# A long convolution and a token mixer on one Trainium2 core: step one's last tile copied in two operations, step two's last sums in halves, and two chunks' sums of group 4 on VectorE

## The chip, the cores and the metric

The kernel runs on one core of a Trainium2 chip. The core has five engines with a queue of instructions each: TensorE (PE, its weight loads shown as PEld), VectorE (DVE), ScalarE (ACT), GpSimd (POOL) and SyncE (SP), which issues most of the transfers between HBM and the on-chip memory SBUF. TensorE writes its results to a second on-chip memory, PSUM, from which VectorE and ScalarE read. The metric is the device time of one launch in microseconds, as the median of several runs.

## The reference

```python
x = A_q                                                   # 2048 tokens, 640 channels
sa, ca, ga, sb, cb, gb = (silu(c) @ w_mod).reshape(6, 640)
h = layernorm(x) * (1 + ca) + sa
k_shift = causal depthwise convolution of A_k with A_shift_k, 4 taps
kv = k_shift * A_v
y = irfft(rfft(kv, 4096) * rfft(A_ssm_k, 4096))[:2048]    # a long causal convolution per channel
x = x + ga * (h * (y + kv * A_ssm_D))
h = layernorm(x) * (1 + cb) + sb
u = gelu(einsum("sd,sf->df", h, B_w1) + B_b1)
out = x + gb * (einsum("df,fs->ds", u, B_w2) + B_b2).T
```

## The kernel before

The 640 channels are worked in five chunks of 128, `c` = 0 to 4 (the loop at L521). A chunk's long convolution is done as products with Fourier matrices on TensorE:

- **Step one**, `step1(side, t)` at L222: sixteen products of a tile of the kv side (`side` 0, from the buffer `X`) or of the ssm_k side (`side` 1, from the buffer `P`) go to one PSUM slot. ScalarE then copies the slot into `Z`, laid out by side, tile, row, column and half. There are four tiles `t` a side, and a tile has 64 columns `k1` for each row.
- **Step two**, `f2(g)` at L236, for eight groups `g` of eight columns: 32 products read the columns 8g to 8g + 7 of all eight tiles of `Z`. ScalarE copies the filter's half of the result to `kt` (L250). Two products on VectorE (`mul`, L254) multiply it with the signal's half into `pa` and `pb`, which lie in `P` and are used by every second group. Two sums (`add`, L260) then make the real and the imaginary part of `Y`, for the eight columns and all 32 rows `i`. The sums are GpSimd's, except those of group 7, which are VectorE's in the chunks from 1 on (L552).
- **Back**, `i2(r)` at L267 and `i1(half)` at L285: `i2(0)` reads the rows 0 to 15 of `Y` in all columns, `i2(1)` the rows 16 to 31; ScalarE (in the last chunk VectorE too, L281) copies the results to `T2`. `i1` gives half of the tokens, and `gate` multiplies them with the normalised input; the result is added to x.

Every engine works off its instructions in the order in which the program issues them; there is no scheduler. In the loop over `g` (L525 to L548) VectorE gets the products of group g - 1, GpSimd (L530) the sums of group g - 2, ScalarE two operations on the input, and VectorE a share of a list `fill`: the short convolution and the product with v for a later chunk, or statistics. After the loop come the products of group 7, the sums of group 6 on GpSimd and the sums of group 7. Then follow, for chunks 1 to 3, two tiles of step one for the next chunk, a copy on ScalarE that permutes ssm_k into `P` (L176), seven operations of `fill`, `i2(0)`, two operations on the whole chunk's input (`po`, L303), further tiles of step one, `i2(1)` and `i1`. Chunk 4 has, in place of the next chunk's work, modulation products (L358) and the first splits of the mixer's weights (L418). In chunks 1 to 3, GpSimd also adds `ssm_D` to a row of ssm_k (L173) after group 3.

PSUM has three slots that go round (`ring`, L69), so group g of step two can write its slot when the products of group g - 3 have read it. A fourth slot holds the running sum of the short convolution and its taps. VectorE's operations of the short convolution read one operand from there and one from SBUF; its sums for `Y` read both operands from SBUF.

From about 292 us on the second normalisation and the token mixer follow, in two large matrix products.

Of the kernel before, what the change touches and what calls it, by code (L numbers as in the profile page):

```python
# [11 lines left out]
AF = mybir.ActivationFunctionType  # L12
ALU = mybir.AluOpType
# [37 lines left out]
def mixer_kernel(ctx: ExitStack, tc: tile.TileContext, q, k, v, shift_k, ssm_k, ssm_D, w1, b1, w2, b2, c,  # L51
# [7 lines left out]
    act, dve, pool, pe, sync = nc.scalar, nc.vector, nc.gpsimd, nc.tensor, nc.sync  # L59
    TT = lambda eng, o, a, b, op: eng.tensor_tensor(o, a, b, op=op)  # L60
# [36 lines left out]
    Z = T_z.rearrange("p (s t a k e) -> p s t a k e", s=2, t=4, a=8, e=2)  # L97
    T2 = T_z[:, 4096:8192].rearrange("p (a m e) -> p a m e", a=32, e=2)
    Y = T_y.rearrange("p (r i k) -> p r i k", r=2, i=32)
# [122 lines left out]
    def step1(side, t, later=False):  # L222

        ps = psum()
        for a in range(8):
            i = 8 * t + a
            lhs = KSP[:, i] if side else X.rearrange("p (m i) -> p i m", i=32)[:, i]
            o = 512 * (a % 2) + 128 * (a // 2)
            for ri in range(2):
                pe.matmul(ps[64 * ri:64 * ri + 64, o:o + 128], lhs, F1[:, 128 * ri:128 * ri + 128], start=True,  # L230
                          stop=True)
        evac = lambda: act.activation(Z[:, side, t].rearrange("p a k e -> p e a k"),  # L232
                                      ps.rearrange("p (e a k) -> p e a k", a=8, e=2), AF.Copy)
        return evac if later else evac()

    def f2(g):  # L236

        ps = psum()
        for kk in range(8):
            k1 = 8 * g + kk  # L240
            for ri in range(2):
                for h in range(2):
                    o = 128 * kk + 64 * ri
                    rhs = bass.AP(tensor=T_z.tensor, offset=T_z.offset + 128 * h + 2 * k1,
                                  ap=[T_z.ap[0], [256, 32], [1, 2]])
                    pe.matmul(ps[64 * h:64 * h + 64, o:o + 64], W2[k1 // 32][:, 2 * (k1 % 32) + ri], rhs, start=True, stop=True)  # L246
        pv = ps.rearrange("p (m s i) -> p m s i", s=2, i=32)
        xs_ = pv[:, :, 0]
        kt = KT[g % 2]
        act.activation(kt.rearrange("p (m i) -> p m i", i=32), pv[:, :, 1], AF.Copy)  # L250
        pa, pb = P[:, 1024 * (g % 2):1024 * (g % 2) + 512], P[:, 1024 * (g % 2) + 512:1024 * (g % 2) + 1024]
        m16 = lambda t: t.rearrange("p (m i) -> p m i", i=32)

        def mul():  # L254
            TT(dve, m16(pa), xs_, m16(kt), ALU.mult)
            sw = bass.AP(tensor=kt.tensor, offset=kt.offset + 32, ap=[kt.ap[0], [64, 8], [-32, 2], [1, 32]])
            TT(dve, pb.rearrange("p (k r i) -> p k r i", k=8, r=2), xs_.rearrange("p (k r) i -> p k r i", r=2), sw,
               ALU.mult)

        def add(eng=pool):  # L260
            for ri, t, op in ((0, pa, ALU.subtract), (1, pb, ALU.add)):
                t = t.rearrange("p (k r i) -> p r i k", k=8, r=2)
                TT(eng, Y[:, ri, :, 8 * g:8 * g + 8], t[:, 0], t[:, 1], op)
        return mul, add


# [254 lines left out]
    for c in range(NC):  # L521
# [3 lines left out]
        for g in range(8):  # L525
# [1 line left out]
            if pend_m:  # L527
                pend_m()
            if pend_a:
                pend_a()  # L530
            pend_a, pend_m = (pend_m and pa_next), m_
            pa_next = a_
            if c:
# [15 lines left out]
        pend_m()  # L549
        if pend_a:  # L550
            pend_a()
        pa_next(dve if c else pool)  # L552
        if c == 0:
            for j in range(16):
                for h in range(2):
# [6 lines left out]
        if c == 0:  # L562
# [3 lines left out]
            ps = psum()  # L566
# [45 lines left out]
        else:  # L612
# [6 lines left out]
            t = mem("in", 4288, "wb3")  # L619
# [4 lines left out]
        if c:  # L624
            dv(7 if cn is not None else 8)
            i2(0)
            if cn is None:
                mod_part(tap, 3, pl[3])
                i2(1, dve)
                t = mem("y", 4096, "wb2")  # L630
# [19 lines left out]
        for half in range(2):  # L650
            ps = i1(half)
# [123 lines left out]
    ps = i1(1, s1)  # L775
# [405 lines left out]
```

## Time and profile before

| | us |
|---|---|
| median of 3 runs | 689.63 (688.66 to 690.23) |
| the profiled execution's own time | 686.98 |
| its span, from the first to the last instruction | 685.2 |
| PE busy | 631.4 |
| DVE busy | 513.5 |
| ACT busy | 313.7 |
| POOL busy | 147.1 |

The page says who was busy and for how long, and its chain of waits says who ended last, followed back from the last instruction. A line of a timeline gives start, length, engine, line, operation, output and inputs, how many instructions were merged, and in brackets the idle time of the engine before and who ended it. Names stand without their numbers: `z` is `Z`, `y` is `Y`, `p` is the buffer `P`, `pst` a PSUM slot. All of VectorE's and GpSimd's two-operand operations have the line of one helper, L60, and are told apart by their tiles. Step two runs at about 42, 104, 157, 206 and 257 us in the five chunks.

### The profile page before, as it was taken

The page shows a single profiled execution, that of the slowest core. Times are in us where ns is not written, and L with a number is a line of the kernel's source. Part 1 is how long each engine was busy: PE and PEld are TensorE (multiplying, and loading weights), DVE is VectorE, ACT ScalarE, POOL GpSimd, SP SyncE. Part 2 cuts the span into 40 slices and gives each one's busy share as a digit, 9 for nine tenths or more (in the row PEclk, how much of TensorE's full clock was granted, in tenths as well). Part 3 has the DMA queues.
Part 4 walks back from the last instruction along what each step waited for, and adds up shares of the span by engine and source line. Part 5 has one row for each costly group of instructions (what it writes and reads, how often), then busy time and mean ns, then how long its engine had stood idle before and what let it go on. Part 6 is the DMA issues. An engine that isn't in the chain of part 4 may idle for free.

```text
span 685.2 us, 20698 instructions
## 1 busy us (share of the span) xinstructions
PE 631.4 (92%) x9057; PEld 613.1 (89%) x9057; DVE 513.5 (75%) x865; ACT 313.7 (46%) x469; POOL 147.1 (21%) x120
## 2 busy tenths in 40 slices
PE   0699888989999989997799999999999999999997
PEld 0699688989999989787799999999999999999997
DVE  7677689969879737888996320774589888888886
ACT  0564674735745645555777321532433332333331
POOL 5298048525526427200000000000000000000000
PEclk9999989999999999989999999999999999999999
DMA  9978988546432623352112750577589563355511
GB/s 184 215 219 242 357 154 173 121 80 147 77 63 85 178 48 81 118 127 60 29 34 57 129 112 12 139 186 193 167 300 347 170 182 103 117 168 170 175 40 40
DMA packets 173552, 95.91 MB, mean 140 GB/s; under 512 B 89715, under 2 KB 163222, under 8 KB 173462
## 3 DMA queue, kind: packets, MB, share of 16 engines
q1 hardware_dynamic: 168914, 93.28, 52.5%
q10 hardware_dynamic: 4548, 1.31, 1.1%
q8 instruction: 71, 1.16, 0.7%
q14 instruction: 19, 0.16, 0.1%
HBM read 77.53 MB, written 17.04 MB: 138 GB/s over the span
## 4 chain that ended last, share of the span: by engine, by line
PE 69%; DVE 15%; POOL 5%; DMA 3%; issue 2%; SPq 2%; ACT 2%; ACTq 0%; POOLq 0%; DVEq 0%
PE pst L1082 25%; PE pst L441 19%; PE pst L230 8%; PE pst L246 6%; PE pst L275 5%; POOL y L60 4%; PE pst L947 3%; DVE tap L60 2%; PE pst L294 2%; DVE kt L60 2%; SPq L166 2%; DMA in<-in_A_k_dram 1%; POOL t L60 1%; DMA aux<-in_A_ssm_k_dram 1%; DVE p L60 1%
## 5 line engine op out<-in xcount | busy, mean ns | idle before, releaser
L246 PEld LDWEIGHTS pst<-z,w 128*64 128x64 f32 x2560 | 94.8, 141 | 9.2 <-ACT z L232 7.3
L246 PE MATMUL pst<-z,w 128*64 128x64 f32 x2560 | 96.0, 240 | 7.5 <-ACT z L232 6.1
L60 POOL TENSOR_TENSOR y<-p 128x256 f32<-128x256 f32 x72 | 92.0, 1339 | 25.0 <-DVE p L60 24.6
L60 DVE TENSOR_TENSOR p<-pst,kt 128x512 f32<-128x512 f32 x80 | 52.5, 693 | 21.0 <-ACT kt L250 15.1
L230 PE MATMUL pst<-v,x 128*64 128x128 f32 x640 | 45.5, 302 | 23.4 <-DVE x L60 23.4
L230 PEld LDWEIGHTS pst<-v,x 128*64 128x64 f32 x640 | 43.6, 221 | 23.9 <-POOL aux L60 23.3
L232 ACT ACTIVATE z<-pst 128x1024 f32<-128x1024 f32 x40 | 46.4, 1165 | 39.3 <-PE pst L230 19.4
L250 ACT ACTIVATE kt<-pst 128x512 f32<-128x512 f32 x40 | 25.1, 628 | 49.5 <-PE pst L246 27.3
L275 PEld LDWEIGHTS pst<-v,y 32*128 32x128 f32 x1280 | 38.0, 187 | 5.4 <-POOL y L60 2.5
L275 PE MATMUL pst<-v,y 32*128 32x64 f32 x1280 | 39.9, 272 | 2.5 <-DVE y L60 1.4
L230 PE MATMUL pst<-v,p 128*64 128x128 f32 x640 | 37.3, 274 | 2.1 <-ACT p L176 1.1
L230 PEld LDWEIGHTS pst<-v,p 128*64 128x64 f32 x640 | 35.0, 137 | 3.1 <-issue 1.5
L1082 PE MATMUL pst<-r_z,m_w 128*128 128x320 f32 x198 | 37.1, 309 | 0.0
L60 DVE TENSOR_TENSOR tap<-tap,kt 128x512 f32<-128x512 f32 x51 | 35.6, 697 | 1.3
L60 DVE TENSOR_TENSOR kt<-in,tap 128x512 f32<-128x512 f32 x51 | 35.0, 687 | 1.5
L1082 PEld LDWEIGHTS pst<-r_z,m_w 128*128 128x128 f32 x198 | 31.1, 188 | 0.0
L283 ACT ACTIVATE z<-pst 128x512 f32<-128x512 f32 x38 | 21.5, 667 | 20.2 <-PE pst L275 20.2
L1019 ACT ACTIVATE m_w<-m_v 128x896 fp32r<-128x896 f32 x19 | 17.9, 948 | 23.3 <-DVE m_v L60 13.1
L294 PEld LDWEIGHTS pst<-z,v 64*64 64x64 f32 x1280 | 22.6, 146 | 6.6 <-issue 3.6
L294 PE MATMUL pst<-z,v 64*64 64x64 f32 x1280 | 24.6, 231 | 3.1 <-issue 2.1
L60 DVE TENSOR_TENSOR m_w<-m_v,m_w 128x896 fp32r<-128x896 f32 x19 | 20.7, 1087 | 6.5 <-ACT m_w L1019 6.5
L60 DVE TENSOR_TENSOR aux<-pst,aux 128x1024 f32<-128x1024 f32 (+2 forms) x11 | 12.3, 1125 | 16.6 <-PE pst L294 16.6
(300 smaller groups left out, 1434.9 us busy)
## 6 DMA issues: line engine op xcount, KB each, us to landing
x<-in_B_w_dram SPq DMA_DIRECT2D x20, 512.0 KB
m_v<-in_B_w_dram SPq DMA_DIRECT2D x20, 384.0 KB
aux<-in_A_ssm_k_dram SPq DMA_DIRECT2D x10, 512.0 KB
out_dram<-m_w SPq DMA_DIRECT2D x32, 160.0 KB
in<-in_A_k_dram SPq DMA_DIRECT2D x36, 128.0 KB
in<-in_A_v_dram SPq DMA_DIRECT2D x36, 128.0 KB
ts<-m_p SPq DMA_DIRECT2D x10, 320.0 KB
m_w<-xs SPq DMA_DIRECT2D x20, 160.0 KB
```

What stands on the lines that cost most here:

```text
L60: TT = lambda eng, o, a, b, op: eng.tensor_tensor(o, a, b, op=op)
L230: pe.matmul(ps[64 * ri:64 * ri + 64, o:o + 128], lhs, F1[:, 128 * ri:128 * ri + 128], start=True, stop=True)
L232: evac = lambda: act.activation(Z[:, side, t].rearrange("p a k e -> p e a k"), ps.rearrange("p (e a k) -> p e a k", a=8, e=2), AF.Copy)
L246: pe.matmul(ps[64 * h:64 * h + 64, o:o + 64], W2[k1 // 32][:, 2 * (k1 % 32) + ri], rhs, start=True, stop=True)
L250: act.activation(kt.rearrange("p (m i) -> p m i", i=32), pv[:, :, 1], AF.Copy)
L275: pe.matmul(pp[qd // 2][:, o:o + 64], Y[p, ri, i:i + 2].rearrange("p i k -> p (i k)"), V2[p, 64 * ri:64 * ri + 64], start=ri == 0, stop=ri ...
L283: act.activation(o, i, AF.Copy)
L294: pe.matmul(ps[64 * b:64 * b + 64, 512 * e + 64 * jj:512 * e + 64 * jj + 64], V1[p, ri, n2], T2[p, :, 32 * ri + n2], start=ri == 0, stop=r ...
L441: pe.matmul(ps[0:m, h, 0:320], w_.bitcast(F32R), r_[:, 320 * h:320 * h + 320].bitcast(F32R), start=first and i == 0, stop=last and i == 2)
L947: pe.matmul(ps[n][:, h, 0:320], sets[n][:, j].bitcast(F32R), r[:, 320 * h:320 * h + 320].bitcast(F32R), start=j == 0 and r is hh, stop=j = ...
L1019: act.activation(W[n][0].bitcast(F32R), A[p, w_], AF.Copy)
L1082: pe.matmul(bank[n], w[:, i].bitcast(F32R), r.bitcast(F32R), start=m == 0 and k == 0, stop=m == 6 and k == 2)
```

## The change

Three edits. First, `step1`'s copy of the ssm_k side's last tile (`side` 1, `t` 3) is made in two operations, columns 0 to 7 and then 8 to 63, in all five chunks. Second, in the chunks from 1 on the sums of group 7 are made for the rows 0 to 15 first, real and imaginary, and then for the rows 16 to 31: four operations on VectorE in place of two. Third, in chunks 2 and 3 the sums that are issued in the loop at `g` = 6, those of group 4, go to VectorE and no longer to GpSimd.

```diff
@@ step1
-        evac = lambda: act.activation(Z[:, side, t].rearrange("p a k e -> p e a k"),
-                                      ps.rearrange("p (e a k) -> p e a k", a=8, e=2), AF.Copy)
+        def evac(cuts=(0, 8, 64) if side and t == 3 else (0, 64)):
+
+            for k0, k1 in zip(cuts, cuts[1:]):
+                act.activation(Z[:, side, t, :, k0:k1].rearrange("p a k e -> p e a k"),
+                               ps.rearrange("p (e a k) -> p e a k", a=8, e=2)[:, :, :, k0:k1], AF.Copy)
         return evac if later else evac()
@@ f2
-        def add(eng=pool):
-            for ri, t, op in ((0, pa, ALU.subtract), (1, pb, ALU.add)):
-                t = t.rearrange("p (k r i) -> p r i k", k=8, r=2)
-                TT(eng, Y[:, ri, :, 8 * g:8 * g + 8], t[:, 0], t[:, 1], op)
+        def add(eng=pool, parts=(slice(0, 32),)):
+            for i in parts:
+                for ri, t, op in ((0, pa, ALU.subtract), (1, pb, ALU.add)):
+                    t = t.rearrange("p (k r i) -> p r i k", k=8, r=2)
+                    TT(eng, Y[:, ri, i, 8 * g:8 * g + 8], t[:, 0, i], t[:, 1, i], op)
@@ the loop over g
             if pend_a:
-                pend_a()
+                pend_a(dve if c in (2, 3) and g == 6 else pool)
@@ after the loop
-        pa_next(dve if c else pool)
+        if c:
+            pa_next(dve, (slice(0, 16), slice(16, 32)))
+        else:
+            pa_next()
```

VectorE at the end of step two in chunk 3, before and after (chunk 2 is alike; `p<-pst` are the two products of a group, `y<-p` its sums, `x<-tap,in` the last operation of `fill`, and the rows behind the sums the statistics of x):

```order
L60 TENSOR_TENSOR p<-pst_3081,kt 128x512 x2
L60 TENSOR_TENSOR x<-tap,in 128x512
L60 TENSOR_TENSOR p<-pst_3122,kt 128x512 x2
L60 TENSOR_TENSOR p<-pst_3163,kt 128x512 x2
L60 TENSOR_TENSOR p<-pst_3203,kt 128x512 x2
L60 TENSOR_TENSOR y<-p 128x32x8 x2
L520 BN_STATS sm<-xa 128x6 x7
```

```order
L60 TENSOR_TENSOR p<-pst_3089,kt 128x512 x2
L60 TENSOR_TENSOR x<-tap,in 128x512
L60 TENSOR_TENSOR p<-pst_3130,kt 128x512 x2
L60 TENSOR_TENSOR y<-p 128x32x8 x2
L60 TENSOR_TENSOR p<-pst_3171,kt 128x512 x2
L60 TENSOR_TENSOR p<-pst_3211,kt 128x512 x2
L60 TENSOR_TENSOR y<-p 128x16x8 x4
L524 BN_STATS sm<-xa 128x6 x7
```

The two sums of group 4 now stand between the products of group 5 and those of group 6, and the sums of group 7 are four operations of 16 rows.

ScalarE at the passage from step one to step two in chunk 4, before and after (`z<-pst` are the copies of step one's tiles, `kt<-pst` the first copy of step two, `aux` the input's normalisation):

```order
L232 ACTIVATE z<-pst_3658 128x2x512
L232 ACTIVATE z<-pst_3676 128x2x512
L250 ACTIVATE kt<-pst_3706 128x512
L301 ACTIVATE aux<-xa,sm 128x128 x2
L538 ACTIVATE x<-sm 128x1
```

```order
L235 ACTIVATE z<-pst_3668 128x2x512
L235 ACTIVATE z<-pst_3686 128x2x8x8
L235 ACTIVATE z<-pst_3686 128x2x8x56
L253 ACTIVATE kt<-pst_3717 128x512
L305 ACTIVATE aux<-xa,sm 128x128 x2
L542 ACTIVATE x<-sm 128x1
```

The last tile's copy is now two operations, of 2 x 8 x 8 and of 2 x 8 x 56 elements a partition, and nothing stands between them.

TensorE at the start of step two in chunk 2, with what each first product of a group waits for, before and after:

```order
L246 MATMUL pst_2129<-z,w_75 64x64 [waits Activation_49]
L246 MATMUL pst_2167<-z,w_75 64x64 [waits PE_49]
L246 MATMUL pst_2207<-z,w_75 64x64 [waits PE_49]
L246 MATMUL pst_2248<-z,w_75 64x64 [waits DVE_49,Activation_49]
L246 MATMUL pst_2291<-z,w_76 64x64 [waits DVE_49,Activation_49]
```

```order
L249 MATMUL pst_2134<-z,w_75 64x64 [waits Activation_49]
L249 MATMUL pst_2172<-z,w_75 64x64 [waits PE_49,Activation_49]
L249 MATMUL pst_2212<-z,w_75 64x64 [waits PE_49]
L249 MATMUL pst_2253<-z,w_75 64x64 [waits DVE_49,Activation_49]
L249 MATMUL pst_2296<-z,w_76 64x64 [waits DVE_49,Activation_49]
```

The second group has a wait for ScalarE that it did not have: the first group waits for the first copy, the second for the second.

## The prediction, made before the changed kernel was run

> **What bounds the kernel now.** I read the page first, its chain of waits above all, then that chain in order of time, then the timeline at each place the change touches. The page gives the span and who holds the chain:
>
> ```profile
> span 685.2 us, 20698 instructions
> PE 69%; DVE 15%; POOL 5%; DMA 3%; issue 2%; SPq 2%; ACT 2%; ACTq 0%; POOLq 0%; DVEq 0%
> ```
>
> The chain in order of time (start, length, what) shows who ends last where:
>
> ```profile
> 76.38 0.37 SPq L574
> ...
> 160.77 1.28 DVE p L60 x2
> ...
> 167.62 10.25 POOL y L60 x8
> ...
> 179.40 1.52 DVE y L60
> 181.05 3.58 PE pst L275 x120
> ...
> 199.79 1.23 DVE aux L60
> ...
> 217.14 10.28 POOL y L60 x8
> ...
> 250.44 5.42 PE pst L230 x96
> 255.93 1.08 ACT z L232
> 257.05 17.78 PE pst L246 x474
> ...
> 358.22 42.50 PE pst L441 x288
> ```
>
> From 358 us to the end PE holds it in products that the change leaves alone, so only what lies before, the five chunks c = 0 to 4, can move. In chunk 2 (and, 217.14 - 167.62 = 49.5 us later, in chunk 3) step two is not PE's: POOL's sums run back to back, VectorE's products wait for them, and i2(0) waits for the last sums on VectorE. In chunk 4 it is PE's, and PE begins it only when ScalarE has copied step one's last tile. The waits of PE from 100 to 292 us (who, for whom: us in total, times, longest) name the two places that the change aims at:
>
> ```profile
> PE pst L246 <- ACT z L232: 4.9, 4, 1.2
> PE pst L275 <- DVE y L60: 1.4, 2, 0.7
> ```
>
> I call the sums of group g a(g), its products m(g); a(7).0 and a(7).1 are its two operations, and h a half of one.
>
> **Part one: the last tile's copy in two.** One copy of 1024 columns becomes one of 128 and one of 896; step two's first group reads the 128 alone. Rows of ScalarE's groups, shapes apart:
>
> ```profile
> L232 ACT ACTIVATE z<-pst 128x1024 f32<-128x1024 f32 x40 | 46.4, 1165 | 39.3 <-PE pst L230 19.4 <-PE pst L294 19.4
> L250 ACT ACTIVATE kt<-pst 128x512 f32<-128x512 f32 x40 | 25.1, 628 | 49.5 <-PE pst L246 27.3 <-ACT aux L301 14.3 <-DVE p L60 3.5
> L301 ACT ACTIVATE aux<-xa,sm 128x128 f32<-128x128 f32 x40 | 17.5, 494 | 1.6 <-DVE sm L347 1.6
> L568 ACT ACTIVATE sm<-pst 128x36 f32<-128x36 f32 x1 | 0.2, 187 | 0.0
> ```
>
> From 512 to 1024 columns a copy grows by 0.54 us, 1.05 ns a column; the same line gives 0.23 at 128. The nearest rows bound it: 0.19 (36 columns from PSUM) and 0.49 (128, with a column of scales). I take 0.25, since a plain copy from PSUM is nearer to the first. PE then starts 1.07 - 0.25 = 0.8 us earlier (0.6 at the bound). The second part, about 1.0 us, ends 1.3 us after the start, while the first group keeps PE for 19.05 / 8 = 2.4 us (row below): hidden, and late by 1 us only if that group were free.
>
> What the 0.8 is worth depends on who ends last behind it:
>
> ```profile
> 69.14 1.07 ACT L232 ACTIVATE z<-pst 128x1024 f32<-128x1024 f32 x1 [0.83 <-PE pst L230]
> 64.49 1.20 SPq L351 DMA_DIRECT2D aux<-in_w_mod_dram  x2
> 77.96 0.69 PEld L358 LDWEIGHTS tap<-aux,sm 128*32 128x32 f32 x12 [1.14 <-DMA aux<-in_w_mod_dram]
> ...
> 101.20:130.00 28.80, 26.23 (x618) 25.18 (x614) 28.18 (x43) 15.51 (x29) 26.13 (x22) 1.00 0.76 162
> ```
>
> - Chunk 0: PE runs into the weights of the modulation, issued at 64.5 behind 32 issues of q by SP and landing at 77.9. SP waits for nothing that moves before 66.5, so these land when they did: 0.
> - Chunk 1: VectorE is busy 28.18 of the 28.80 us from 101.2 to 130.0 (third figure of the row); it sets this step two: 0.
> - Chunks 2 and 3: the first products start at 160.77 behind VectorE's backlog (in the chain VectorE stands ahead of them, not PE, from the gate at 199.79 on in chunk 3); PE's lead is eaten there: 0.
> - Chunk 4: here everything starts with PE.
>
> ```profile
> 257.05 19.05 PE L246 MATMUL pst<-z,w 128*64 128x64 f32 x512 [1.23 <-ACT z L232]
> 260.42 1.29 DVE L60 TENSOR_TENSOR p<-pst,kt 128x512 f32<-128x512 f32 x2 [5.04 <-ACT kt L250]
> 261.19 17.92 POOL L60 TENSOR_TENSOR y<-p 128x256 f32<-128x256 f32 x14 [6.97 <-DVE p L60]
> ```
>
> VectorE idled 5.04 us before m(0), POOL 6.97 before a(0): both move with PE. The term is 0.8.
>
> **Part two: the last sums in halves.** The operations concerned, and the POOL operation that runs beside them (duration min/median/max in ns, first and last start):
>
> ```profile
> L60 DVE TENSOR_TENSOR y<-p x2: 976/1242/1509, 178.5 to 179.4; 128x256 f32<-128x256 f32 x2
> L60 POOL TENSOR_TENSOR y<-p x2: 1177/1366/1554, 177.8 to 178.9; 128x256 f32<-128x256 f32 x2
> ...
> L60 DVE TENSOR_TENSOR y<-p x2: 610/1053/1496, 278.1 to 279.5; 128x256 f32<-128x256 f32 x2
> L60 POOL TENSOR_TENSOR y<-p x1: 1145/1145/1145, 278.0 to 278.0; 128x256 f32<-128x256 f32 x1
> ```
>
> POOL's last operation ends at 178.9 + 1.55 = 180.45, VectorE's at 179.4 + 1.51 = 180.91, 0.46 later; in chunk 4 the first on VectorE ends at 278.1 + 1.50 = 279.6, 0.45 after POOL's at 279.15. So such an operation on VectorE stands still while one of POOL's runs, then needs 0.46 (0.61 at most, the row's minimum). POOL's operation beside it is stretched in turn: 1.55 against 1.15. They take turns. At 1.05 ns an element (128 fewer) a half costs 0.46 - 0.13 = 0.33; bounds 0.3 and 0.61.
>
> [...]
>
> i2(0) needs the first halves and all of POOL's a(6). PE's rows, and ScalarE's beside them:
>
> ```profile
> 129.60 4.11 PE L275 MATMUL pst<-v,y 32*128 32x64 f32 x128
> 79.17 3.80 PE L275 MATMUL pst<-v,y 32*128 32x64 f32 x128
> 180.99 2.09 ACT L176 ACTIVATE p<-aux 128x2048 f32<-128x2048 f32 x1
> 184.65 2.26 ACT L283 ACTIVATE z<-pst 128x512 f32<-128x512 f32 x4 [1.57 <-PE pst L275]
> ```
>
> Chunk 1: 4.11 us against 3.80 unhindered; POOL's last operation still has to pass between the two first halves, so of these 0.3 I count 0.2. The second halves follow 0.66 behind the first, in chunk 2 (below) at 180.8, where a(7) ended at 180.91: ScalarE's permutation (180.99), which overwrites the products, is not put off and still done before i2(0)'s results come at 184. Were it later by a microsecond, the copies at 184.65 would be late next, and i2(1) with them.
>
> **Part three: a(4) on VectorE in chunks 2 and 3.** It takes two of the ten operations from POOL and queues two on VectorE ahead of m(6) and m(7); those free PSUM slots for PE's next tiles. POOL and VectorE in chunk 2:
>
> ```profile
> L60 POOL TENSOR_TENSOR y<-p x10: 1092/1372/1554, 167.6 to 178.9; 128x256 f32<-128x256 f32 x10
> 173.04 0.71 DVE L60 TENSOR_TENSOR p<-pst,kt 128x512 f32<-128x512 f32 x1 [0.29 <-POOL y L60]
> 175.77 4.20 PE L230 MATMUL pst<-v,x 128*64 128x128 f32 x63
> ```
>
> One of POOL's takes 1.28 from start to start ((178.9 - 167.6 + 1.55) / 10), 1.09 at the quickest, 1.37 in the median; the one at 177.8, beside the same neighbours that a(5) will have, took 1.18, and I go by 1.2. VectorE's m(5) starts its second half at 173.04, when a(3) is out, and ends at 173.7. Taking turns from there: a(5).0 on POOL 173.0 to 174.2; a(4).0 on VectorE to 174.67; a(5).1 to 175.87; a(4).1 to 176.34; m(6) to 177.65; m(7) to 178.9; a(6) on POOL from 177.1 to 179.5; two halves to 180.16. i2(0) starts at 180.25 and ends 3.80 later, 184.05, where it ended at 181.05 + 3.58 = 184.63: 0.6. With 1.09 it is 0.95, with 1.28 0.3. The tile of step one whose PSUM slot waits for m(6) starts at 177.7 and takes 4.20 / 2 = 2.1, so PE is ready at 179.8 and covers it; were m(6) later, PE would be late next. Behind i2(0), PE leads to the gate (199.79) and that to VectorE's backlog of chunk 3, so the gain passes on. Chunk 3 alike: 0.6.
>
> Chunk 4 keeps a(4) on POOL. Its end, with 0.8 earlier from part one:
>
> ```profile
> 279.74 4.11 PE L275 MATMUL pst<-v,y 32*128 32x64 f32 x128 [0.27 <-ACT wb L418]
> 283.63 4.89 DVE L60 TENSOR_TENSOR aux<-aux,g 128x1024 f32<-128x1024 f32 x4
> 288.95 1.29 DVE L281 TENSOR_SCALAR z<-pst 128x512 f32<-128x512 f32 x2 [0.43 <-PE pst L275]
> ```
>
> POOL ends at 278.3, four halves at 279.65, where the sums ended at 280.1. VectorE then has 8.4 us of splits and products (280.1 to 288.52), so it is free at 288.05; PE has i2(0) from 279.1 to 282.9 and i2(1) 5.05 later, at 287.95 (both ran 283.85 to 288.9). VectorE's copy starts at 288.05 and not at 288.95: 0.9, of which 0.8 is part one's; what is left of i2(0)'s lead waits behind VectorE.
>
> **The sum.** 0.2 + 0.6 + 0.6 + 0.9 = 2.3 us. The profiled execution took 686.98 us (span 685.2 and 1.8 around it); the median is 689.63, 2.65 above. The difference carries over: 684.7 in a profile alike, a span of 682.9, and a median of **687.3**.
>
> **The rivals.**
> - Chunk 0's 0.8 passes after all, because the loads that SP issues at 76.4 carry chunk 1: 686.5. For it: that issue stands in the chain, behind PE. Against: VectorE's chain starts from the modulation rows, behind 77.96. Chance 0.10.
> - POOL needs its median, 1.37, beside a(4) as well: the turns then put m(6)'s end at 178.0, a(6)'s at 180.15 and i2(0) at 180.9 to 184.7, and chunks 2 and 3 gain nothing. 0.2 + 0.9 = 1.1: 688.5. For it: most of the ten were that slow. Against: the undisturbed one at 177.8 was not. Chance 0.13.
> - [...] Chance 0.09.
> - Slower: every sum on VectorE, halves too, meets a POOL operation and takes the longest seen, 1.51. In chunk 2 a(4) ends at 176.7, m(7) at 179.35, the first halves at 182.4: 1.7 lost, in chunk 3 too; chunk 1 loses 0.45, chunk 4's queue ends 2.9 late. 6.7 in all: 696.3. It turns to a loss where a half is over 0.8. Against: POOL has nothing left to run after a(6). Chance 0.08.
> - That the tiles' ranges aren't told apart, so that step two waits for both copies, is excluded: group one and group two wait for ScalarE separately in the changed order.
>
> **How the numbers follow.** The forecast has 0.60. A change of 0.2%, 1.4 us, is about what a measurement of this kernel tells from none. Faster by more: 0.95 of the forecast, the first rival and a third of the second, 0.57 + 0.10 + 0.04 = 0.71; slower by more: 0.08; the rest, 0.21, within. The range goes from all bounds together in favour (0.3 + 0.95 twice + 1.0 + 0.8 = 4.0, 685.6) to 689.5, a little over the second rival, for the median's own drift; the third rival and the slower one, 0.17 together, lie outside.
>
> **What would show it.** Right: step two's first group starts about 0.3 us behind the start of the last tile's copy in all chunks; in chunks 2 and 3 POOL's second run has eight operations and i2(0) starts with no break, some 0.6 us earlier against m(0); chunk 4's copy at L281 comes 0.9 us earlier against f2's old start. Wrong: a first copy over 0.5 us; halves over 0.6; m(6) ending over 4.5 us behind m(5) in chunk 2; or PE waiting after step one's second tile for something new.

## The result and the profile after

The changed kernel takes 687.11 us in the median of 20 runs (684.26 to 697.42), the kernel before 689.98 of 20 (686.38 to 700.87). The ratio is 0.9948, with a 95% interval of 0.993 to 0.9965: 3.6 us faster, 2.4 to 4.8. The medians are of all runs, while ratios and mean clocks here and below leave out the runs that took over 1.5% more than the fastest of their kernel; the two medians alone are 2.9 us apart. The profiled execution of the changed kernel, however, took 688.47 us and is longer than the one of before (686.98), so the two profiles do not show the gain at their ends. The page of the changed kernel, span and chain of waits:

```profile
span 686.7 us, 20717 instructions
PE 69%; DVE 19%; DMA 3%; issue 3%; POOL 3%; ACT 2%; SPq 0%; ACTq 0%; DVEq 0%; POOLq 0%
```

POOL's share of the chain fell from 5% to 3%, VectorE's rose from 15% to 19%. In chunk 2 the chain now leaves POOL at 172.5 us, goes through VectorE's products and the sums a(4), and reaches i2(0) by step one's second tile. PE's waits from 100 to 295 us (us in total, times, longest) show the same change from PE's side:

```profile
PE pst L230 <- DVE p L60: 2.2, 2, 1.1
...
PE pst L249 <- ACT z L235: 1.7, 4, 0.4
PE pst L298 <- issue: 1.6, 2, 1.2
PE pst L279 <- issue: 0.6, 1, 0.6
```

The wait for the last tile's copy is down from 1.2 to 0.4 us each, and the one of i2(0) for the sums is gone from the list. The first row is new: step one's second tile waits 1.1 us in chunks 2 and 3 for the products m(6), which are queued behind the sums a(4) on VectorE. The last row is new too, and it is a pause that follows from no wait.

The timeline of the changed kernel (start, length, engine and line, [idle before]), first chunk 2, then chunk 4:

```profile
154.67 1.22 ACT L235 ACTIVATE z<-pst 128x128 f32<-128x128 f32 x2 [0.60 <-PE pst L230]
155.00 19.03 PE L249 MATMUL pst<-z,w 128*64 128x64 f32 x511 [0.44 <-ACT z L235]
159.69 1.31 DVE L60 TENSOR_TENSOR p<-pst,kt 128x512 f32<-128x512 f32 x2
168.45 0.69 DVE L60 TENSOR_TENSOR p<-pst,kt 128x512 f32<-128x512 f32 x1 [0.72 <-POOL y L60]
172.52 0.70 DVE L60 TENSOR_TENSOR p<-pst,kt 128x512 f32<-128x512 f32 x1 [0.76 <-POOL y L60]
173.13 2.74 DVE L60 TENSOR_TENSOR y<-p 128x256 f32<-128x256 f32 x2
177.22 2.33 PE L230 MATMUL pst<-v,x 128*64 128x128 f32 x32 [1.06 <-DVE p L60]
178.19 1.74 DVE L60 TENSOR_TENSOR y<-p 128x128 f32<-128x128 f32 x4
179.47 3.80 PE L279 MATMUL pst<-v,y 32*128 32x64 f32 x128
...
254.13 1.22 ACT L235 ACTIVATE z<-pst 128x128 f32<-128x128 f32 x2 [0.62 <-PE pst L230]
254.46 19.05 PE L249 MATMUL pst<-z,w 128*64 128x64 f32 x512 [0.44 <-ACT z L235]
...
276.91 3.87 PE L279 MATMUL pst<-v,y 32*128 32x64 f32 x128
281.91 2.12 PE L279 MATMUL pst<-v,y 32*128 32x64 f32 x65
284.65 2.85 PE L279 MATMUL pst<-v,y 32*128 32x64 f32 x63 [0.62 <-issue]
287.57 1.29 DVE L285 TENSOR_SCALAR z<-pst 128x512 f32<-128x512 f32 x2 [1.51 <-PE pst L279]
```

Step two begins 0.33 us behind the start of the copy in both chunks (155.00 - 154.67, 254.46 - 254.13), where it was 1.12 in chunk 4 (257.05 - 255.93). i2(0) runs in one piece of 3.80 us in chunk 2. The trace lists each of these fp32 products as two records (i2(0) issues 64 products, its row counts 128), and the counts below are of records. In chunk 4 i2(1) breaks off for 0.62 us, and the 63 records behind the break take 2.85 us where the 65 ahead of it took 2.12. So each chunk can be read from the start of that copy to the end of i2(0):

| copy of the last tile to the end of i2(0), us | chunk 1 | 2 | 3 | 4 |
|---|---|---|---|---|
| before | 30.63 | 28.91 | 28.95 | 27.92 |
| changed | 30.23 | 28.60 | 28.54 | 26.65 |
| difference | -0.40 | -0.31 | -0.41 | -1.27 |
| predicted | -0.2 | -0.6 | -0.6 | -0.9 |

These make 2.4 us, against the predicted 2.3. Between the end of i2(0) and the next chunk's copy another 1.5 us went in chunk 1's tail (22.00 to 20.50), 0.3 in chunk 2's, and 0.2 came back in chunk 3's, so that the segment from the end of chunk 1's i2(0) to that of chunk 4's, called S below, fell from 150.13 to 146.61 us. Chunk 1's tail had two breaks of PE with no wait behind them before (0.93 and 0.80 us), and one of 0.43 after.

Most of what the profiled execution lost, it lost at the clock. Windows of 3.4 us of the changed kernel around the break in chunk 4 (busy times and counts by engine, then the granted clock, DMA share, GB/s):

```profile
282.30:285.70 3.40, 2.78 (x100) 2.74 (x99) 3.33 (x4) 0.72 (x2) 0.00 (x0) 0.99 0.04 12
285.70:289.10 3.40, 3.40 (x46) 2.19 (x42) 1.65 (x3) 1.59 (x4) 0.00 (x0) 0.50 0.02 5
289.10:292.50 3.40, 3.40 (x110) 2.79 (x108) 1.29 (x2) 1.28 (x3) 0.00 (x0) 0.51 0.02 5
```

For 6.8 us PE runs at half clock, right behind the break. Chunk 0 has more of it than before (a mean of 0.83 from 60 to 100 us, 0.91 before), and the chain of waits in order of time shows what hangs on it there:

```profile
73.60 5.80 PE tap L362 x40
79.69 10.68 DMA aux<-in_A_ssm_k_dram
```

A load that chunk 1 needs is issued only when PE's modulation products are through. In the profile before, PE left the chain at 76.4 us, here at 79.4. From the end of chunk 4's i2(0) to the end of the span the profile before needs 401.35 us, this one 405.9. Of these 4.5 us, 3.4 are lost by the end of chunk 4's i1. The rest goes in the token mixer, whose last products alone took 0.9 us longer (173.57 us against 172.64) with no half clock in them; why is open.

### The profile page after: what moved, and what is told of

The parts are those of the page before. It is cut to its first block, busy times and chain, and to the rows that moved or that the text cites. A ratio compares the mean times of both kernels' runs of the same rounds, so it can differ in the third digit from the quotient of the medians.

```text
span 686.7 us, 20717 instructions
## 1 busy us (share of the span) xinstructions
PE 635.6 (93%) x9057; PEld 615.2 (90%) x9057; DVE 516.4 (75%) x877; ACT 314.2 (46%) x474; POOL 142.9 (21%) x116
## 4 chain that ended last, share of the span: by engine, by line
PE 69%; DVE 19%; DMA 3%; issue 3%; POOL 3%; ACT 2%; SPq 0%; ACTq 0%; DVEq 0%; POOLq 0%
PE pst L1089 24%; PE pst L445 17%; PE pst L230 9%; PE pst L249 6%; PE pst L279 5%; DVE tap L60 4%; PE pst L954 3%; DVE kt L60 3%; POOL y L60 2%; PE tap L362 2%; DVE p L60 2%; PE pst L298 2%; DMA aux<-in_A_ssm_k_dram 2%; DVE x L60 1%; DMA m_v<-in_B_w_dram 1%
## 5 line engine op out<-in xcount | busy, mean ns | idle before, releaser
L60 POOL TENSOR_TENSOR y<-p 128x256 f32<-128x256 f32 x68 | 88.8, 1359 | 24.1 <-DVE p L60 23.8
L230 PE MATMUL pst<-v,x 128*64 128x128 f32 x640 | 45.3, 298 | 25.7 <-DVE x L60 23.5
L235 ACT ACTIVATE z<-pst 128x1024 f32<-128x1024 f32 (+2 forms) x45 | 46.8, 1052 | 41.9 <-PE pst L230 24.2
L279 PEld LDWEIGHTS pst<-v,y 32*128 32x128 f32 x1280 | 40.0, 195 | 3.9 <-issue 1.9
L279 PE MATMUL pst<-v,y 32*128 32x64 f32 x1280 | 41.6, 281 | 1.3 <-ACT z L235 0.6
L1089 PE MATMUL pst<-h_x,m_w 128*128 128x320 f32 x132 | 24.9, 310 | 0.4 <-DVE h_x L60 0.4
```

Of the source, the lines that this page charges most:

```text
L235: act.activation(Z[:, side, t, :, k0:k1].rearrange("p a k e -> p e a k"), ps.rearrange("p (e a k) -> p e a k", a=8, e=2)[:, :, :, k0:k1], ...
L279: pe.matmul(pp[qd // 2][:, o:o + 64], Y[p, ri, i:i + 2].rearrange("p i k -> p (i k)"), V2[p, 64 * ri:64 * ri + 64], start=ri == 0, stop=ri ...
L1089: pe.matmul(bank[n], w[:, i].bitcast(F32R), r.bitcast(F32R), start=m == 0 and k == 0, stop=m == 6 and k == 2)
```

## The experiments

Each run is timed beside the kernel before on the same chip. The mean clock is that of the kernel's timed runs; it was 0.983 for the kernel before and 0.987 for the changed one. S is from one profile each.

| run | median, us | ratio to before (95%) | mean clock | S, us |
|---|---|---|---|---|
| changed kernel | 687.11 | 0.9948 (0.993 to 0.9965) | 0.987 | 146.61 |
| cut alone | 691.98 | 1.0015 (0.9984 to 1.0046) | 0.977 | 153.72 |
| halves alone | 688.19 | 0.997 (0.9945 to 0.9994) | 0.986 | 149.37 |
| sums alone | 687.58 | 0.9964 (0.994 to 0.9988) | 0.988 | 148.38 |
| halves and sums | 687.98 | 0.9953 (0.9926 to 0.9979) | 0.987 | 148.50 |
| cut and halves | 689.00 | 0.9987 (0.9953 to 1.002) | 0.981 | 150.67 |
| cut and sums | 686.17 | 0.9934 (0.9903 to 0.9964) | 0.989 | 148.14 |
| cut alone, wait filled with 16 | 691.09 | 1.0029 (1.0008 to 1.005) | 0.985 | 153.32 |
| cut alone, wait filled with 4 | 689.74 | 1.0006 (0.9977 to 1.0036) | 0.983 | 150.85 |
| changed, chunk 0 filled | 687.18 | 0.997 (0.9945 to 0.9995) | 0.990 | 145.16 |
| changed, group 2's sums | 685.14 | 0.9931 (0.9904 to 0.9958) | 0.985 | 144.01 |
| the same, in chunk 4 too | 688.22 | 0.999 (0.9956 to 1.0023) | 0.984 | 147.28 |
| group 2's sums, cut in chunk 4 alone | 687.54 | 0.9956 (0.993 to 0.9983) | 0.985 | 148.21 |

### Each edit alone

**The cut alone.** The other two edits are taken back:

```diff
-                pend_a(dve if c in (2, 3) and g == 6 else pool)
+                pend_a()
-            pa_next(dve, (slice(0, 16), slice(16, 32)))
+            pa_next(dve)
```

> The first edit alone. Stage theory: the lead of 0.8 us shows in all five chunks between the start of the last tile's copy and step two's first product (1.15 us before, about 0.35 now), but is kept only in chunk 4; in chunks 2 and 3 the stretch from the first product on VectorE to the end of i2(0) stays at 23.9 us; the whole is 0.8 us faster, ratio 0.9988. Rival, chunk 0 passes: VectorE's first operation of chunk 1 comes 0.8 us earlier too, 1.6 us in all, ratio 0.9977. Rival, the cut is the whole gain: ratio 0.995.

It gained nothing (1.0015), though step two starts 0.33 us behind the copy in every chunk. Both rivals lie outside the interval. The stage theory's 0.9988 lies within it, but the 23.9 us that it expected in chunks 2 and 3 became 26.51 and 26.14. The timeline of PE in chunk 2, before and then in this kernel, and windows of 3.4 us of this kernel there:

```profile
179.89 0.45 PE L275 MATMUL pst<-v,y 32*128 32x64 f32 x8
181.05 3.58 PE L275 MATMUL pst<-v,y 32*128 32x64 f32 x120 [0.71 <-DVE y L60]
```

```profile
177.56 0.45 PE L279 MATMUL pst<-v,y 32*128 32x64 f32 x8 [0.54 <-DVE y L60]
178.99 6.06 PE L279 MATMUL pst<-v,y 32*128 32x64 f32 x120 [0.97 <-DVE y L60]
```

```profile
176.40:179.80 3.40, 1.88 (x46) 1.61 (x45) 3.37 (x5) 1.98 (x2) 1.98 (x2) 0.99 0.00 0
179.80:183.20 3.40, 3.40 (x72) 3.40 (x69) 3.23 (x6) 1.19 (x1) 0.00 (x0) 0.50 0.23 41
183.20:186.60 3.40, 3.40 (x52) 3.28 (x50) 3.37 (x3) 1.54 (x4) 0.00 (x0) 0.50 1.12 180
186.60:190.00 3.40, 3.40 (x48) 3.07 (x44) 1.73 (x1) 1.77 (x3) 0.00 (x0) 0.51 0.63 102
```

PE is ready earlier, the sums are not. So it waits 0.54 us ahead of i2(0) and 0.97 within it, where it waited 0.71 within it and not ahead of it before. Behind this pause the clock is granted at half for 10.2 us, and the 120 records take 6.06 us instead of 3.58. Chunk 3 does the same (pauses of 0.60 and 0.97 us, then 5.64). In all, S is 3.6 us longer than before. In chunk 4, where no such pause stands, the 0.8 us is there: VectorE's copy at the end starts 32.16 us behind the copy of the last tile, where it was 33.02.

**The halves, and the sums, alone:**

```diff
-        def evac(cuts=(0, 8, 64) if side and t == 3 else (0, 64)):
+        def evac(cuts=(0, 64)):
```

and of the other two edits one is taken back as above.

> The second edit alone. Stage theory: VectorE's first halves still wait for GpSimd's last sum, so in chunks 2 and 3 the stretch from the first product on VectorE to the end of i2(0) goes from 23.9 to about 23.6 us, and chunks 1 and 4 win 0.1 to 0.2 each: 0.8 us in all, ratio 0.9988. Rival, a half costs as much as a whole (0.61 us): no chunk wins, chunk 4 loses 0.6, ratio 1.0005. Rival, the halves are most of the gain: ratio 0.996.

> The third edit alone, group 4's sums on VectorE in chunks 2 and 3, group 7's sums whole. Stage theory: GpSimd is done earlier, but step one's second tile on TensorE now waits about 1 us for group 6's products, and the two whole sums behind group 7's products end where they did: the stretch from the first product to the end of i2(0) is 23.7 to 24.0 us (23.9 before), ratio 0.9995 to 1.0003. Rival, as the prediction priced it: 0.6 us won in each of the two chunks without the halves, ratio 0.998.

PE's i2(0) of chunk 2, of the first kernel and then of the second:

```profile
183.04 3.58 PE L279 MATMUL pst<-v,y 32*128 32x64 f32 x120 [0.30 <-DVE y L60]
```

```profile
182.11 4.07 PE L279 MATMUL pst<-v,y 32*128 32x64 f32 x128
```

The halves take the wait within i2(0) from 0.71 to 0.30, and i2(0) ends 0.37 us earlier behind m(0) in chunk 2 and 0.45 in chunk 3. The sums alone take the wait away, and i2(0) ends 0.46 and 0.52 us earlier, at 23.40 us behind m(0) in both, earlier than the 23.7 expected at best. Neither needs the cut. The times tell less. The halves' ratio, 0.997, has both the theory's 0.9988 and the second rival's 0.996 in its interval, and only the first rival is out; the trace, at 23.49 and 23.47 us, is the theory's 23.6. The sums' ratio, 0.9964, excludes the theory (0.9995 to 1.0003) and agrees with the rival, the prediction's price.

**Halves and sums, without the cut:**

> The second and third edits without the first. Stage theory: chunks 2 and 3 as in the changed kernel, 23.5 us from the first product to the end of i2(0), and step two of chunk 4 starts 1.15 us behind the start of the last tile's copy as before; 1.2 us faster than the kernel before, ratio 0.998, and 0.8 us slower than the changed kernel. Rival, the cut does everything: ratio 1.000. Rival, the cut does nothing: ratio 0.995, as the changed kernel's.

i2(0) ends 0.75 and 0.82 us earlier behind m(0) in chunks 2 and 3, at the quickest 3.80 us, and the ratio, 0.9953, can't be told from the changed kernel's. The theory's 0.998 lies just outside the interval, and 0.995, the rival by which the cut does nothing, within it: by the times alone the cut is not seen to add anything. The timeline of VectorE's waits for POOL in its chunk 2 shows what the cut does there:

```profile
172.45 0.69 DVE L60 TENSOR_TENSOR p<-pst,kt 128x512 f32<-128x512 f32 x1 [0.20 <-POOL y L60]
174.93 0.70 DVE L60 TENSOR_TENSOR p<-pst,kt 128x512 f32<-128x512 f32 x1 [0.36 <-POOL y L60]
181.86 3.80 PE L279 MATMUL pst<-v,y 32*128 32x64 f32 x128
```

Here VectorE waits 0.6 us in all for POOL to give back the products' buffers; in the changed kernel, with the groups coming earlier, 2.1 us (the 0.72 and 0.76 above among them), and m(5) ends 13.53 us behind m(0) instead of 13.08. The wait has its source on POOL: its first four sums of the chunk take 5.78 us in chunks 2 and 3 of the changed kernel and 5.09 here, 5.75 to 5.86 in all kernels in which these chunks have the cut (but for chunk 2 of one, 5.21) and 5.05 to 5.30 in all others. So POOL loses 0.7 us where the groups come earlier, nearly the lead itself. That is why the changed kernel has 0.28 and 0.42 us left of the 0.75 and 0.82 in chunks 2 and 3.

### Is it the pause that costs the cut its gain?

**Filling it.** 16 products that nothing reads ahead of i2(0) of chunks 2 and 3, in the kernel with the cut alone:

```diff
+        for n in range(warm):
+            pe.matmul(pp[0][:, 0:128], F1[:, 0:128], F1[:, 0:128], start=True, stop=True)
-            i2(0)
+            i2(0, warm=16 if c in (2, 3) else 0)
```

> The first edit alone again, and 16 matrix multiplications of 128 x 128, whose results nothing reads, ahead of i2(0) in chunks 2 and 3, where TensorE waits for step two's last sums. Theory (the clock): the cut alone brought its lead of 0.8 us, and lost more than that because TensorE's pause ahead of i2(0) fell almost whole into one stretch of 3.4 us, behind which the clock was granted at half for 10.2 and 6.8 us. With the pause filled these two stretches are gone, m(0) to the end of i2(0) falls from 26.5 and 26.1 us to 23.5 to 24.0, the mean clocks rise from 0.977 to 0.983 or more, and the time falls by about 2 us, to 689 to 690. Rival (the cut itself): the second of the two copies ends later than the one did, and what reads it pays; then the pause was not the cause, and the time stays at 691 to 693.

```profile
187.78 3.83 PE L275 MATMUL pst<-v 128*128 128x128 f32 x32
191.54 3.80 PE L281 MATMUL pst<-v,y 32*128 32x64 f32 x128
```

PE's timeline in chunk 2: the fill took 3.83 us, 0.24 a product, far more than meant, and put i2(0) 1.5 us behind the last sums (which ended at 190.02). But i2(0) runs at full clock in both chunks, 3.80 us, and the mean clock is 0.985 instead of 0.977. The profiled execution itself was a long one (700.16 us, with 20.5 us at half clock in chunk 0), so only these two places are read from it. The expected 689 to 690 us and 23.5 to 24.0 us behind m(0) did not come (691.09, and 26.03 and 26.02), since each of the two chunks paid 1.5 us for the fill. So the fill keeps the clock, and the size was wrong. With 4 instead:

> The first edit alone, with 4 of the unread 128 x 128 products ahead of i2(0) in chunks 2 and 3 instead of 16: those 16 took 3.83 us, 0.24 us each, where TensorE waited for 1.5 us, and put off i2(0) of each of the two chunks by 1.5 us. 4 of them, 0.96 us, fit into the wait. Theory (the clock): no stretch at half clock behind i2(0) in chunks 2 and 3, m(0) to the end of i2(0) 23.5 to 24.0 us, a mean clock near 0.985, and the cut's 0.8 us shows: a ratio of 0.997 to 1.000. Rival (the cut itself costs): m(0) to the end of i2(0) over 24.5 us without a stretch at half clock, or a ratio of 1.001 or more at a mean clock no lower than that of before.

```profile
180.16 1.16 PE L275 MATMUL pst<-v 128*128 128x128 f32 x8
181.97 5.52 PE L281 MATMUL pst<-v,y 32*128 32x64 f32 x128 [0.65 <-DVE y L60]
...
234.36 3.58 PE L281 MATMUL pst<-v,y 32*128 32x64 f32 x120 [0.72 <-DVE y L60]
```

Chunk 3 (last row) kept its clock (120 records in 3.58 us), with 0.72 us of pause left; chunk 2 lost it behind a pause of 0.65 (0.50 from 184.4 to 191.2 us). The mean clock is that of before, and the ratio, 1.0006, lies between the two expectations: inconclusive on the time.

**Cut with one of the others.** These two complete the set:

> First and second edit, no sums moved. From the end of chunk 1's i2(0) to that of chunk 4's took 150.13 us before, 153.72 with the cut alone, 149.37 with the halves alone, 148.50 with halves and sums, 146.61 in the changed kernel. Theory (a pause at one place is what costs): the cut makes TensorE ready 0.8 us earlier ahead of i2(0), the halves take about 0.4 us from the wait there, so the pause stays under that of the cut alone but near it; in chunks 2 and 3 at most one stretch at half clock is left, the segment takes 147.5 to 150 us, and the time lies between the cut's and the halves', 687 to 690. Rival (the cut has no worth): 149.4 us or more without any stretch at half clock between 150 and 280 us.

> First edit and the moved sums, no halves. Theory: with the sums on VectorE TensorE waits about 1 us for m(6) ahead of its second tile, one pause in two places instead of one, so that no stretch at half clock follows in chunks 2 and 3: the segment takes 146.5 to 148 us, against 153.72 with the cut alone and 148.38 with the sums alone, and the time is 686 to 688. Rival (the cut costs of itself): the segment takes 148.4 us or more, and the time is no lower than with the sums alone (ratio 0.9964).

Windows of the kernel with cut and halves, chunk 2:

```profile
177.70:181.10 3.40, 2.31 (x73) 2.23 (x76) 3.33 (x7) 2.34 (x2) 1.17 (x1) 0.98 0.01 2
181.10:184.50 3.40, 3.40 (x65) 3.28 (x64) 3.26 (x5) 0.85 (x2) 0.00 (x0) 0.50 0.40 66
184.50:187.90 3.40, 3.40 (x32) 3.10 (x31) 3.37 (x3) 2.13 (x4) 0.00 (x0) 0.51 1.20 193
```

PE's timeline of the kernel with cut and sums, chunk 2:

```profile
177.55 2.33 PE L230 MATMUL pst<-v,x 128*64 128x128 f32 x32 [1.07 <-DVE p L60]
179.81 4.01 PE L279 MATMUL pst<-v,y 32*128 32x64 f32 x128
```

With the halves PE still pauses 0.49 and 0.76 us around the start of i2(0), and the clock falls to half for 6.8 us, in chunk 3 likewise; the ratio is 0.9987. The theory expected at most one such stretch and S of 147.5 to 150; there are two, and S is 150.67. The time, 689.00, lies between the cut's and the halves', as expected. With the sums PE waits 1.07 us ahead of the second tile and not at all ahead of i2(0), no stretch follows in either chunk (the granted clock is 1.00 from 150 to 250 us), and the ratio is 0.9934. Its S, 148.14, is just outside the 146.5 to 148 expected, and hardly below the sums' alone, so the cut's part of this gain is not in S alone.

### What the first chunk, and another choice of sums, are worth

**Chunk 0 filled:** 8 unread products ahead of its i2(0), 20 ahead of the first modulation row.

> The changed kernel with 8 matrix multiplications of 128 x 128 that nothing reads ahead of chunk 0's i2(0), and 20 ahead of the first modulation row, where TensorE waits 0.64 and 1.61 us in chunk 0. Theory (the clock follows TensorE's pauses): the stretches at half clock at about 70 and 87 us are gone, i2(0) of chunk 0 takes 4 to 5 us from its first to its last product instead of 6.2, the first i1 of chunk 0 3.3 instead of 4.1, and the mean clock rises by 0.006 to 0.01. What that is worth: if chunk 0's lead does not pass through VectorE's taps (the step of the prediction), the time stays within 0.3 us of the changed kernel's; if it passes, it falls by about 2 us. Rival: the clock falls for another reason than the pauses, and both stretches stay.

```profile
67.66 2.05 PE L275 MATMUL pst<-v 128*128 128x128 f32 x16
69.64 3.80 PE L281 MATMUL pst<-v,y 32*128 32x64 f32 x128
```

The stretch at half clock behind i2(0) is gone: 3.80 us where the changed kernel needed 5.16 for 124 of its 128 records. The second stretch is not gone: it comes at 92 us and is 3.4 us long instead of 6.8. The mean clock, 0.990, is the highest of all, but 0.003 above the changed kernel's and not the 0.006 to 0.01 expected. The median is the changed kernel's, the ratio, 0.997, is somewhat higher, and the intervals overlap. The second fill took 4.9 us where 1.6 were free, so chunk 0's i1 came 3 us later, and what chunk 0 is worth can't be read from this run.

**Group 2's sums instead of group 4's:**

```diff
-                pend_a(dve if c in (2, 3) and g == 6 else pool)
+                pend_a(dve if c in (2, 3) and g == 4 else pool)
```

> The changed kernel, with the sums of group 2 (those of two operations earlier) on VectorE in chunks 2 and 3 instead of the sums of group 4. Theory (VectorE is late at the end): in the changed kernel TensorE's second tile of step one waits 1.06 us for m(6), because VectorE's sums stand right ahead of it. With the sums two groups earlier, m(6) ends about 2.4 to 2.8 us behind m(5) instead of 3.85, the wait is gone, and the end of i2(0) comes 0.3 to 0.5 us earlier behind m(0) in chunks 2 and 3; at an equal clock the time is 0.6 to 1.0 us below the changed kernel's. Rival (POOL): POOL had its break there already, stays the last, and i2(0) ends as in the first edit's kernel, 24 us or more behind m(0). Rival (the clock): without the wait at the second tile the pause lies ahead of i2(0) in one piece, a stretch at half clock follows it in chunk 2 or 3, and the time is 688 to 690.

PE's timeline of this kernel, chunk 2 and chunk 4:

```profile
174.83 4.30 PE L230 MATMUL pst<-v,x 128*64 128x128 f32 x64
...
282.97 3.53 PE L279 MATMUL pst<-v,y 32*128 32x64 f32 x63 [0.72 <-issue]
```

The 1.06 us wait of the second tile is gone, both tiles run in one piece of 4.30 us, and i2(0) ends 22.64 and 22.72 us behind m(0) in chunks 2 and 3 (changed kernel: 23.58 and 23.50), twice what was expected. No stretch at half clock followed in these chunks (i2(0) took 4.13 and 3.87 us there, where 120 of its 128 records took 6.06 and 5.64 with the cut alone). S is the shortest of all, 2.6 us below the changed kernel's. In chunk 4 a break of 0.72 us came within i2(1), with half clock behind it (0.50 from 283.2 to 290.0 us). At 685.14 us (9 runs) and 0.9931 it is the lowest time of the study; its interval overlaps the changed kernel's, so it is ahead by its trace and not by its times.

**The same in chunk 4 too** (`c in (2, 3, 4)`):

> The changed kernel with the sums of group 2 on VectorE, as in the run with group 2's sums in chunks 2 and 3, and in chunk 4 too. There POOL works without a break from the first sums to the last (14 operations in 18.00 us, 2.57 us a group, where TensorE gives a group every 2.38 us), and ends 1.0 us behind m(7). Theory (POOL is the last in chunk 4): with one group fewer POOL waits for m(6) and ends at most 0.5 us behind m(7); the first whole of VectorE's halves no longer waits for it, i2(0) of chunk 4 starts 0.5 to 0.8 us earlier behind the first group, and the time is 0.5 to 0.8 us below that run's (ratio to before 0.991 to 0.9925). Rival (VectorE): its 2.6 us of sums push the statistics that stand between the products past m(6) or m(7), these come later, and chunk 4 gains nothing or loses up to 1 us.

```profile
265.70 3.25 DVE L60 TENSOR_TENSOR y<-p 128x256 f32<-128x256 f32 x2
271.45 2.53 PE L249 MATMUL pst<-z,w 128*64 128x64 f32 x64 [1.07 <-DVE p L60]
```

VectorE's and PE's rows: the rival held, and chunk 4 lost 1.7 us where it allowed for 1. The sums cost VectorE 3.25 us, the products behind them came late, the last group of step two waited 1.07 us for its slot, and i2(0) ended 24.77 us behind m(0) instead of 23.04. In chunk 4 POOL has to keep its sums although it works without a break.

**Group 2's sums, and the cut in chunk 4 alone:**

```diff
-            step1(1, t)
+            step1(1, t, cut=cn == NC - 1)
```

> The run with group 2's sums on VectorE, with the last tile's copy cut in chunk 4 alone and whole in chunks 0 to 3. Theory (the prediction's step: in chunks 1 to 3 VectorE's row of taps sets when m(0) comes, so the lead is worth nothing there): the segment from chunk 1's i2(0) to chunk 4's takes 144.0 to 144.6 us as it did with the cut in all chunks (144.01), and the ratio to before is 0.992 to 0.9945. Rival (the lead counts in each chunk): 145.5 us or more, 0.8 us a chunk for chunks 2 and 3, and a ratio of 0.995 or more.

```profile
157.78 16.68 PE L249 MATMUL pst<-z,w 128*64 128x64 f32 x448 [1.24 <-ACT z L235]
169.48 3.25 DVE L60 TENSOR_TENSOR y<-p 128x256 f32<-128x256 f32 x2
174.01 7.17 POOL L60 TENSOR_TENSOR y<-p 128x256 f32<-128x256 f32 x6 [1.87 <-DVE p L60]
```

The rival held again by S: 148.21 us, not 144.0 to 144.6; the ratio, 0.9956, is on its side, with an interval that reaches the theory's. With the copy whole, the groups come later against VectorE's row. Its two sums meet POOL's and take 3.25 us (2.62 with the cut), m(4) is late, and POOL then waits 1.87 us. Of the 4.2 us between the two values of S, 2.2 lie in chunks 2 and 3 and 1.2 in chunk 1's tail. So the lead is used in chunks 2 and 3 here. The collision is not the whole copy's alone, though: in chunk 2 of the kernel with group 2's sums in chunk 4 too, which has the cut, the two sums took 3.46 us and i2(0) ended 23.29 us behind m(0) instead of 22.64.

## Why the prediction was right, and where it was not

**The time and the sum.** The forecast was 687.3 us from a sum of 2.3; 687.11 was measured, and the chunks' terms make 2.4 in the trace. That both fit so closely is partly luck: the gain against the kernel before is 3.6 us by the ratio, of which the forecast has 2.3, and the terms missed by 0.2 to 0.4 us each, two up and two down. Chunk 1's tail gave another 1.5 us that no term has. Over 263 runs of the study, all those of the ratios for which a clock is on record, a kernel's time rises by 3.5 us for each 0.01 that its mean clock falls. With that one slope and a constant for each kernel, the changed kernel is 2.3 us (plus or minus 0.75) below the kernel before at an equal clock, and its clock, 0.987 against 0.983, accounts for 1.3 more. The same reckoning gives -0.6 for the cut, -0.3 for the halves, -0.7 for the sums and -1.1 for halves and sums at an equal clock (each plus or minus 0.9), -2.0 for cut and halves, -1.7 for cut and sums, and a clock term of +2.1 for the cut alone. Averaged over the four pairs of kernels that differ in one edit alone, the cut is worth 1.1 us at an equal clock, the halves 0.6 and the sums 0.7 (each plus or minus 0.6), against the 0.8 and 1.5 of the sum for the cut and for halves and sums together. This is a correlation over runs, most of which have no trace; the mechanism is shown only in the profiles above.

**Part one, the cut: the size was right, the places partly.** Its 0.8 us is 0.79 in chunk 4 (1.12 to 0.33), where the first copy takes 0.28 us (0.25 reckoned), and it arrives there at the end of i2(0), 1.27 us with the halves. "Chunks 2 and 3: PE's lead is eaten there: 0" was right about m(0), which comes 5.02 us behind the copy's start in chunk 2 (5.05 before), and wrong as a rule. There the lead costs: VectorE waits for POOL (2.1 us, 0.6 in the kernel with halves and sums and no cut), whose first four sums take 0.7 us longer. It costs far more where PE then pauses ahead of i2(0) and the clock falls (cut alone: 0.50 for 10.2 us in chunk 2). And with group 2's sums it is worth something (S of 144.01 with it, 148.21 without it in chunks 1 to 3). Chunk 0's term stays open: the chain there runs through PE and then a load, which speaks for the first rival (686.5), but half clock moved PE's end in it by 3 us, so 0.8 can't be seen.

**Part two, the halves: right.** A half takes 0.36 to 0.41 us where POOL is out of the way, against 0.33 reckoned with bounds of 0.3 and 0.61, and the first one in chunk 2 ends 0.28 us behind POOL's last operation (179.01 and 178.73). The turns that the prediction read from these ends fit every profile here: a sum on VectorE during which POOL's ends is done 0.23 to 0.28 us behind it if it is a half, 0.46 to 0.66 if it is a whole.

**Part three, the sums: right in kind, too large in the changed kernel.** Of the 0.6 in each of chunks 2 and 3, 0.31 and 0.41 arrived. The step that was mis-sized is the place of m(6): reckoned to end 16.9 us behind m(0) (177.65 - 160.77), it ended 17.4 behind (177.07 - 159.69), because m(4) and m(5) wait for POOL, which falls behind once the groups come earlier (m(5) ends 13.53 us behind m(0), reckoned 12.9). "PE is ready at 179.8 and covers it; were m(6) later, PE would be late next" is what happened: PE's second tile waited 1.06 us, and i2(0) followed it without a break. Without the cut the term was 0.75 and 0.82, so it was too small there.

**Chunk 4's 0.9 at VectorE's copy was not there in the profile of the changed kernel.** That copy starts 33.44 us behind the copy of the last tile, 33.02 before: i2(0) ended 1.27 us earlier, and the break of 0.62 us in i2(1) and the half clock behind it took all of it. Where no break stands there the predicted gain is seen: it is 32.21 with cut and sums, and 31.85 in the kernel with chunk 0 filled, whose chunk 4 is the changed kernel's, 1.2 us earlier than before with VectorE never idle ahead of the copy. No term of the sum held the clock.

**"The difference carries over" is the step that failed.** It gave a span of 682.9 us for a profile alike; the profile has 686.7. A profile of this kernel depends on how many stretches at half clock fell into it: up to 350 us the one of before has 17.1 us at half clock, this one 27.3.

**The rivals.** POOL at its median (688.5) is near what chunks 2 and 3 did. POOL's operations beside a(4) did take 1.46 and 1.56 us, but most of the delay was there before them, at m(5). Halves as dear as wholes (0.61 us, the row's minimum), and every sum beside one of POOL's, fell with the 0.37 us; the latter showed itself in chunk 4, with group 2's sums there.

## What to carry to other kernels

An earlier start ahead of a wait for something that does not move only makes the wait longer (0.71 us at chunk 2's i2(0) became 0.54 and 0.97). Here the first edit needed the third: alone it left TensorE those two pauses, behind which the granted clock was 0.50 for 10.2 us, and with the sums moved the same lead paid (the ratio goes from 1 to 1.0015 alone, from 0.997 to 0.9987 on the halves, from 0.9964 to 0.9934 on the sums; none of these steps is clear of its interval by itself). Where edits act on one wait, measure them in all combinations, and compare two kernels by the segments of their traces and at an equal clock, not by the ends of two profiles. Where TensorE had to wait in these traces, 1.06 us ahead of step one's second tile left the granted clock at 1.00; at i2(0), 0.71 us left it there in the kernel before, and 0.65 us did not in the one with 4 to fill.

## What the runs showed of the hardware that was not expected

**Half clock behind short pauses.** The granted clock is 0.5 for 6.8 us (10.2 in chunk 2 of the cut alone) behind pauses of PE of 0.54 + 0.97 us (cut alone), 0.49 + 0.76 (cut and halves) or 0.62 (chunk 4 of the changed kernel, within i2(1)). But a pause of 1.06 us ahead of step one's second tile left the clock at 1.00, and so did this pause in the kernel before, at the start of chunk 2's step two (windows as above):

```profile
155.10:158.50 3.40, 2.15 (x54) 1.91 (x52) 3.26 (x5) 1.09 (x2) 0.00 (x0) 1.00 0.90 227
158.50:161.90 3.40, 3.40 (x99) 3.40 (x97) 3.30 (x6) 1.43 (x4) 0.37 (x1) 1.00 0.49 118
```

PE was busy for 2.15 of 3.40 us there, less than the 2.31 behind which the kernel with cut and halves lost its clock. So neither the pause's length nor the window's share alone decides. Windows of 3.4 us that hold such a pause, and the granted clock of the 3.4 us behind each:

| window from, us | PE busy, us | pauses of PE in it, us | clock behind it |
|---|---|---|---|
| cut alone, chunk 2, 176.40 | 1.88 | 0.54 and 0.97, at i2(0) | 0.50 |
| cut and halves, chunk 2, 177.70 | 2.31 | 0.49 and 0.76, at i2(0) | 0.50 |
| cut, 4 to fill, chunk 2, 181.00 | 2.69 | 0.65, ahead of i2(0) | 0.50 |
| changed, chunk 4, 282.30 | 2.78 | 0.62, within i2(1) | 0.50 |
| group 2's sums, chunk 4, 279.80 | 2.68 | 0.72, within i2(1) | 0.50 |
| changed, chunk 2, 174.90 | 2.34 | 1.06, ahead of step one's second tile | 1.00 |
| before, chunk 2, 155.10 | 2.15 | 1.25, ahead of step two | 1.00 |
| before, chunk 2, 177.90 | 2.69 | 0.71, within i2(0) | 1.00 |
| before, chunk 3, 229.50 | 2.69 | 0.70, within i2(0) | 1.00 |

The five behind which the clock fell lie at i2, but so do the last two, which kept it with 2.69 us busy: the place alone does not decide either. What does was not shown.

**Breaks of PE with no wait behind them** ("issue") come at places in the program that move with an edit. In chunk 1's tail they stand ahead of 24 records of step one and of 24 of i1 in all five kernels whose copy is whole there (before: 0.93 and 0.80 us), and ahead of 25 of i1 alone in eight of the nine with the cut (changed: 0.43). That tail takes 21.7 to 22.0 us in the five and 20.5 to 21.1 in the nine, so the breaks are worth about 1 us there; what makes them was not tried.
